# Zero-tile products on TensorE in thin stretches, later first loads of the MLP weights, and new order constants for head sets 25 to 39, in a transformer block scheduled by its own planner

## The chip, the cores and the metric

One core of one Trainium2 chip. The metric is device microseconds of one execution. The kernel before took 816.97 us (median of 3 runs, 816.37 to 817.6).

## The reference

One adaLN-conditioned transformer block on 2048 tokens of width 640, all in bf16: layer norm, an attention of 32 heads of width 20, and a bilinear gated MLP of inner width 1536. Six vectors of width 640 made from the condition c shift, scale and gate the two halves.

```python
mod = (silu(c) @ w_mod).reshape(1, 6, 1, 640)
sa, ca, ga, sb, cb, gb = mod[:, 0..5]
h = layernorm(x) * (1 + ca) + sa
q, k, v = heads(h @ wqkv)                   # 32 heads of 20
o = softmax(q k^T / sqrt(20)) v
x = x + ga * (o @ wo)
h = layernorm(x) * (1 + cb) + sb
x = x + gb * (((h @ w_gate) * (h @ w_up)) @ w_down)
```

## The kernel before

**Tiles.** Heads go in eight sets of four; the queries go in five chunks (CHUNKS: 512, 512, 512, 256, 256). A pair of chunk and set is an item, called a head set here: 40 of them, numbered 0 to 39 in the order in which they run. Items 0 to 23 belong to the 512-query chunks, 24 to 31 to the first 256-query chunk, 32 to 39 to the second. Scores are products of 32 rows of KT with QT (L1443, four row tiles of the array side by side), written to PSUM with keys on partitions. Most score tiles go through ScalarE, one exp over two or three banks at a time (L1479, into PP). Some, in groups of four called quads, go through VectorE by an arithmetic exp: four bank reads (L1503, into DB), then two masks and one product over 2048 columns (L1535, L1543, L1540, into DSS). QUADS says how many quads each item has. The value products (L2000, four column tiles of 32 columns) add all of an item into one PSUM bank, the value-product bank BPV. When an item is done, VectorE transposes that bank (L1627), takes a reciprocal (L1631), GpSimd scales (L1633), VectorE transposes again (L1641, into OcT), and small DMAs on SP's queue move the rows to Ocp (L1654).

**Per chunk, a suffix.** When its eight items are done, a chunk goes through the output projection (wo with Ocp, L906; L902 in the last chunk), residual, layer norm, transposes (L1758), gate and up products with weights loaded from DRAM into three stage buffers (stg, loads at L1798), their product (hprod) and the down projection (wd with hprod). This work is spread between the scores of the next chunk. The last chunk's suffix comes after the last scores.

**What sets the order.** A planner in the kernel file (class Sched) simulates the engines with costs of its own, picks what each engine does next, and so writes one fixed instruction order per engine; every engine then runs its list in order and waits on semaphores. SP's queue is such a list too: DMA issues stand behind each other. A DMA may have a gate, a number of score groups that must have started before it may be picked; gb is the number of the first group of the next chunk. For TensorE, pick_pe chooses: scores first, then, if recent activity in the planner's account of the last 3413 ns (HAM_W) is under FILL_MIN, other work, then value products in batches, then MLP and projection work, and last a fill: four identity products into a free bank (do_fill, L2329). Each item can set constants of its own (STAGE): batch sizes of value products (PVMIN, PVMAX, PVCAP), how long to hold for a score (HOLD, X_LATE), how far ahead quads are scored (DL, D_LATE, D_RES, EAGER) and FILL_MIN. Constants of item n hold while TensorE's value products are those of item n; DL of an item moves the due places of its own quads.

**Names that the steps touch.** KPB: staging of query rows on their way to DRAM (cast at L1178, written by L1212 to q_rows) and back (L1234, into QT). The stage loads of chunk 0 (L1798) have gate gb - 10. The first product that needs them starts at 268.3 us.

Of the kernel before, what the change touches and what calls it, by code (L numbers as in the profile page):

```python
# [8 lines left out]
BF16 = mybir.dt.bfloat16  # L9
# [7 lines left out]
PV_W = 216.0  # L17
# [100 lines left out]
class Sched:  # L118

    def __init__(self):  # L120
        self.tasks = []
        self.order = {k: [] for k in ("sp", "act", "pe", "dve", "pool")}
        self.all = []
        self.free_at = {k: T0 for k in self.order}
        self.pend = {k: [] for k in self.order}
        self.readyl = {k: [] for k in self.order}
        self.t = 0.0
        self.n = 0
        self.progress = 0
        self.dma_free = 0.0  # L130
        self.pe_mode = None
        self.pe_end = 0.0
        self.pick_pe = None
        self.every = []
        self.ham_w = 0
        self.ham_act = 0.0
        self.cold = True
        self.ncold = 0
        self.nfill = 0
        self.ndup = 0  # L140
        self.nsteal = 0
        self.nx = 0
        self.ng = 1 << 30
        self.hist = []
        self.acts = []
        self.left = 0
        self.lk_end = {"dve": 0.0, "pool": 0.0}
        self.lk_last = None
# [172 lines left out]
def emit_program(nc, sched, nsem_dma=56):  # L321
# [83 lines left out]
    with nc.Block() as block:  # L405
# [20 lines left out]
        def _(e):  # L426
# [5 lines left out]
QUADS = ((0, 4, 3, 3, 3, 3, 4, 4),  # L432
         (3, 4, 2, 4, 3, 4, 4, 4),
         (3, 3, 4, 4, 3, 4, 4, 4),
         (1, 2, 1, 2, 2, 1, 1, 1),
         (1, 1, 1, 1, 1, 1, 1, 1))
D_LEAD = 0.451
NB0, NSS = 2, 3
# [47 lines left out]
GATE_F = (0.468, 0.693, 0.969, 0.732, 1.0)  # L486
FILL_MIN = 4153.722
FILL_HARD = 0.0
FILL_T0, FILL_TH, FILL_MINH = 2300.0, 17000.0, 7500.0
FILL_MODE = 'P'  # L490
DUP_MIN = 0.0
# [37 lines left out]
    22: {"PVMAX": 7, "FILL_MIN": 3913.503, "D_RES": 17, "X_LATE": -76.434, "EAGER": 6, "D_LATE": 16, "PVCAP": 13},  # L529
    23: {"PVTOL": 247, "PVMAX": 7, "D_RES": 23},  # L530
    24: {"PVCAP": 13, "PVMAX": 7, "PVMIN": 2, "FILL_MIN": 4085.526, "DL": 0.464, "EAGER": 7, "STEAL_GAP": 200, "HOLD": 231},
    25: {"STEAL_GAP": 200, "HOLD": 144, "X_LATE": 22.894, "D_RES": 10, "FILL_MIN": 4068.834, "DL": 0.549, "PVCAP": 15, "D_LATE": 14},
    26: {"D_RES": 15, "X_LATE": -39.384, "PVMAX": 9, "PVCAP": 14, "STEAL_GAP": 200, "DL": 0.411},
    27: {"DL": 0.473, "D_LATE": 6, "PVMAX": 6, "EAGER": 6, "D_RES": 75, "PVTOL": 249, "PVMIN": 2, "X_LATE": -47.659},
    28: {"PVCAP": 13, "HOLD": 166, "X_LATE": 82.94},
    29: {"PVCAP": 14, "EAGER": 5, "PVMAX": 7, "D_RES": 46},
    30: {"X_LATE": -110.495, "PVCAP": 15, "FILL_MIN": 3782.61, "D_LATE": 16, "PVTOL": 292},
    31: {"D_RES": 19, "FILL_MIN": 4905.173, "D_LATE": 15, "PVMIN": 2, "X_LATE": 36.868},
    32: {"PVMIN": 2, "D_LATE": 17, "D_RES": 78},
    33: {"STEAL_GAP": 199.702, "D_LATE": 18, "PVCAP": 14, "PVMAX": 4, "DL": 0.442, "PVTOL": 353, "D_RES": 17, "PVMIN": 2, "HOLD": 100},  # L540
    34: {"X_LATE": 150, "D_LATE": 22, "HOLD": 117},
    35: {"PVMIN": 2, "PVMAX": 8, "FILL_MIN": 4516.564, "STEAL_GAP": 179.748, "X_LATE": -53.091, "HOLD": 151, "D_LATE": 12, "PVCAP": 14},
    36: {"PVMIN": 2, "D_RES": 10, "DL": 0.524, "X_LATE": -6.364, "FILL_MIN": 4156.61, "PVMAX": 8, "HOLD": 33},
    37: {"D_LATE": 12, "PVTOL": 254, "PVCAP": 13, "FILL_MIN": 4699.279},
    38: {"D_RES": 60, "PVMAX": 7, "PVTOL": 450, "HOLD": 67, "D_LATE": 16},
    39: {"FILL_MIN": 3000, "D_LATE": 17, "PVTOL": 258, "X_LATE": -54.236, "PVCAP": 16},
}
XHALF = 1
X_LATE = -24.052
X_HALF = 0.0  # L550

# [9 lines left out]
def build_kernel(nc, A_x, A_wqkv, A_wo, B_x, B_w_gate, B_w_up, B_w_down, c, w_mod, out):  # L561
# [29 lines left out]
    def alloc(name, shape, dtype):  # L591
        off = cur[0]
        cur[0] += nb(shape, dtype)
        assert cur[0] <= nc.sbuf_top, f"SBUF overflow at {name}: {cur[0]} > {nc.sbuf_top}"
        return at(name, shape, dtype, off)
# [25 lines left out]
    ident = alloc("ident", [128, 128], BF16)  # L621
    mhalf = alloc("mhalf", [128, 4], F32)
    warm = alloc("warm", [128, 1], F32)
    qcol = alloc("qcol", [128, 1], F32)
    c5 = alloc("c5", [KD, 128], BF16)
    csb = alloc("csb", [128, KD], BF16)
# [125 lines left out]
    def dve(dur, f, deps=(), prio=3.0, **k):  # L752
        return sc.add(Task("dve", dur, f, deps, prio=prio, **k))
# [6 lines left out]
    def pool(dur, f, deps=(), prio=3.0, **k):  # L760
        t = Task("pool", dur, f, deps, prio=prio, **k)
        t.lk = 1
        return sc.add(t)
# [63 lines left out]
    def load_rest():  # L827
# [5 lines left out]
        for q, f in enumerate((first2[0], first2[1],  # L833
# [13 lines left out]
    p_id = pool(300, lambda e: e.affine_select(ident[:], ident[:], pattern=[[-1, 128]], compare_op=ALU.not_equal,  # L847
                                               fill=1.0, base=0, channel_multiplier=1), [p_i0], prio=0)
    p_mh = pool(100, lambda e: e.memset(mhalf[:], -0.5), prio=1)
    p_on = dve(600, lambda e: e.memset(Vf[:, :].rearrange("p (h w) -> p h w", w=VW)[:, :, 0:1], 1.0), prio=-1)  # L850
    d_pz = dve(500, lambda e: e.memset(ps[:, BPV, :], 0.0), [], prio=3.5)
    d_wz = [dve(70, lambda e, w=w: e.memset(w[:, :, D:WKQ], 0.0), prio=0) for w in (wk_sb, wq_sb)]
# [824 lines left out]
    def suffix(ci):  # L1677
# [24 lines left out]
        def pr(early=False):  # L1702
            return pbase + rc_[0] - (1500 if tail and early else OPFIRST if early else 0)
        d_xc = dma("sp", 128 * ntl * D * 2, lambda e: e.dma_start(xck[:, 0:ntl, :], xv[:, t0:t0 + ntl, :]),
                   (first if alt else bd.get("out", []) + v_last), prio=15, gate=max(0, gb - 20))
        t_xn2 = []
        x1_done = []
        op_last = []
# [80 lines left out]
        for fc in range(FT):  # L1789
            use_x = tail and fc < nsx  # L1790
            wbuf, dm = [], []
            for w_, wv in enumerate((wgv, wuv)):
                cell = {}
                if use_x:
                    cell["t"] = stx[fc][:, w_, :, :]

                def f(e, wv=wv, fc=fc, cell=cell):
                    return e.dma_start(cell["t"], wv[:, :, fc * 128:(fc + 1) * 128])  # L1798
                t = dma("sp", 2 * 128 * KD * 128 * 2, f, sfx_done["qdead"] if use_x and fc < nsq else first if use_x else kp_use if ci == 0 else [], prio=16 + ci + .01 * fc,
                        gate=int(gstart[NC] - 40) if tail and not use_x else 0 if tail else max(0, gb - 10))  # L1800
                if not use_x:
                    t.acq = [(sStg[w_], "s", 1)]

                    def on0(task, cell=cell, w_=w_):
                        cell["i"] = task.slots["s"]
                        cell["t"] = stg[cell["i"]][:, w_, :, :]
                    t.on_start = on0
                wbuf.append(cell)
                dm.append(t)
# [112 lines left out]
    def mode_start(mode, t):  # L1922
        if sc.pe_mode is not None and sc.pe_mode != mode:
            return max(t, sc.pe_end + (PE_BACK if sc.pe_mode == 'S' else PE_SWITCH))
        return max(t, sc.pe_end)

    def s_ready():
        g = pvstate["sidx"]
        if g >= NG:
            return None  # L1930
        ts, us = score_q[g]
        r = 0.0
        for d in ts.deps:
            if d.done is None:
                return None
            r = max(r, d.done + SEM)
        for pool, key, refs in ts.acq:
            a = pool.avail()
            if a is None:
                return None  # L1940
            r = max(r, a[0])
        return r
# [265 lines left out]
    def pick_pe(t):  # L2208
# [99 lines left out]
        if cands and not js and len(cands) >= 2 and (not PV0 or it >= PV0N or len(cands) >= PV0 or cands[0][0] == 'd'):  # L2308
            pv_issue(cands, t)
            return True  # L2310
        if t > FILL_T0 and fill_ok(t, fill_deps):
            return do_fill(t)
        return False

    def do_fill(t):
        mode = FILL_MODE if pvstate["sidx"] else "X"
        start = mode_start(mode, t)
        fs = G
        if pvstate["sidx"] == 0:
            fs = next((q for q in (GX, GC) if q.avail() is not None and q.avail()[0] <= t), GC)  # L2320
        task = Task("pe", 216.0, ffill, fill_deps, ctr="pex", mode=mode, name="fill", acq=[(fs, "g", 1)])
        if not sc.acquire(task, t):
            return False
        b_ = task.slots["g"]
        idb = ident[:].unsqueeze(1).to_broadcast([128, 4, 128])
        if mode == "X":
            task.emits = [lambda e: e.matmul(ps[:, b_, :].rearrange("p (a b) -> p a b", a=4), ident[:], idb)]  # L2327
        else:
            task.emits = [lambda e, x=x: e.matmul(  # L2329
                ps[32 * x:32 * x + 32, b_, :].rearrange("p (a b) -> p a b", a=4), ident[:, 32 * x:32 * x + 32], idb,  # L2330
                tile_position=(0, 32 * x), skip_group_check=True) for x in range(4)]
        sc.activity(start, 512.0)
        sc.left += 1
        sc.finish_issue(task, start, 216.0 * clk())
        fs.done(b_, task)
        sc.pe_mode = mode
        sc.pe_end = start + 216.0 * clk()
        sc.free_at["pe"] = sc.pe_end
        sc.nfill += 1
        return True  # L2340
# [4 lines left out]
    def fill_ok(t, fdeps):  # L2345
        if any(d.done is None or d.done + SEM > t for d in fdeps):
            return False
        if xcur[0] is not None and not (PASSDEP or HT0_SPLIT):
            return False
        return sc.recent(t) < (FILL_MINH if t < FILL_TH else FILL_MIN)  # L2350
# [54 lines left out]
```

## Time and profile before

| | |
|---|---|
| Runs without profile | 816.97 us (816.37 to 817.6) |
| Profiled execution, first to last instruction | 821.3 us (the only time that is known of it) |
| ScalarE busy | 775.3 us, 94% |
| TensorE busy | 793.6 us, 97% (matmuls overlap, their ends are modelled) |
| VectorE busy | 720.4 us, 88% |
| Mean granted TensorE clock | 0.988 |
| exp on ScalarE (L1479) | 677 over two banks (1120 ns mean), 98 over three (1523 ns) |
| VectorE's read of a bank (L1503) | 400, 682 ns mean |
| masks and product of a quad (L1535, L1543, L1540) | 706, 690 and 1226 ns mean |
| identity fills (L2329) | 300 matmuls in groups of four |

The page's second part cuts the span into 40 slices with the busy share of each engine in tenths; the row PEclk is the granted clock of TensorE. The groups of part 5 give busy time, the mean of one, and the idle time ahead of them with what ended it. A line of the timeline gives start, length, engine, line, operation, tiles, count of merged instructions, and in brackets the idle time ahead with its releaser; SPq is the issue of a DMA by SP. A line of the windows view gives for a stretch its length, then for PE, PEld, DVE, ACT and POOL the busy time and count, then granted clock, DMA share and GB/s.

### The profile page before, as it was taken

What the parts mean: (1) busy time and instruction counts of PE and PEld (TensorE: products, weight loads), DVE (VectorE), ACT (ScalarE), POOL (GpSimd) and SP (SyncE); (2) the same over time, 40 slices, a digit from 0 to 9 for tenths busy, and PEclk for the clock granted to TensorE, in tenths of its full rate; (3) what the DMA queues carried; (4) which work ended last, traced back from release to release, by engine and by line L of the source; (5) the groups of instructions that cost most, each with busy time, mean ns of one, the idle gap of its engine ahead of it and who ended that gap; (6) DMA issues with size and microseconds to landing.
All of it is one profiled execution on the core that took longest, in us unless ns stands there. A gap on an engine that the chain in (4) does not pass through costs nothing.

```text
span 821.3 us, 28879 instructions
## 1 busy us (share of the span) xinstructions
PE 793.6 (97%) x12493; PEld 305.9 (37%) x12493; DVE 720.4 (88%) x1275; ACT 775.3 (94%) x818; POOL 79.1 (10%) x105
## 2 busy tenths in 40 slices
PE   9999999999989999999999999999988999999998
PEld 4433333322223223233233232333143444554567
DVE  7989999899989999999999999998798877667753
ACT  6899999999989999999999999999899999999941
POOL 3300000020002000000011000000011000001000
PEclk9999999999999999999999999999699999999999
DMA  9734211114500235000300222000400236105610
GB/s 292 219 85 104 67 45 40 50 33 123 131 18 25 54 99 138 22 11 23 92 7 6 53 54 54 6 21 23 82 8 10 50 87 134 47 30 127 137 42 17
DMA packets 116445, 54.71 MB, mean 67 GB/s; under 512 B 83915, under 2 KB 116319, under 8 KB 116319
## 3 DMA queue, kind: packets, MB, share of 16 engines
q1 hardware_dynamic: 115391, 51.72, 24.9%
q8 instruction: 99, 1.62, 0.8%
q10 hardware_dynamic: 928, 1.15, 0.4%
q14 instruction: 27, 0.22, 0.1%
HBM read 41.85 MB, written 8.41 MB: 61 GB/s over the span
## 4 chain that ended last, share of the span: by engine, by line
PE 43%; ACT 35%; DVE 15%; issue 7%; DMA 0%; SPq 0%; POOL 0%; DVEq 0%; ACTq 0%; POOLq 0%
ACT PP L1479 34%; PE ps_all L1443 13%; PE ps_all L906 13%; PE ps_all L2000 9%; DVE DB L1503 5%; PE ps_all L902 3%; DVE DSS L1540 3%; DVE DSS L1543 2%; DVE DSS L1535 1%; PE ps_all L2327 1%; PE ps_all L1166 1%; PE ps_all L1102 1%; PE ps_all L1063 1%; DVE wd L1429 1%; DVE gsb L1847 1%
## 5 line engine op out<-in xcount | busy, mean ns | idle before, releaser
L1479 ACT ACTIVATE PP<-ps_all 128x1024 bf16<-128x1024 f32 (+1 forms) x775 | 756.2, 1171 | 11.6 <-PE ps_all L1443 10.0
L1443 PE MATMUL ps_all<-QT,KT 32*128 32x512 bf16 (+1 forms) x2560 | 311.4, 343 | 16.6 <-ACT PP L1479 10.9
L1503 DVE TENSOR_SCALAR DB<-ps_all 128x512 int16<-128x512 f32 x400 | 265.0, 682 | 43.7 <-PE ps_all L1443 42.9
L1443 PEld LDWEIGHTS ps_all<-QT,KT 32*128 32x128 bf16 x2560 | 81.3, 91 | 264.9 <-ACT PP L1479 228.4
L2000 PE MATMUL ps_all<-PP,Vf 128*32 128x512 bf16 (+2 forms) x2084 | 166.0, 346 | 0.4 <-DVE OT L1627 0.4
L1540 DVE TENSOR_TENSOR DSS<-DB,DSS 128x2048 bf16<-128x2048 bf16 x100 | 122.6, 1226 | 0.0
L906 PE MATMUL ps_all<-h2T,stg 128*32 128x512 bf16 (+1 forms) x1740 | 116.8, 347 | 0.9 <-DVE DB L1503 0.2
L1633 POOL TENSOR_TENSOR OTn<-OT,invT 128x512 bf16<-128x512 f32 (+1 forms) x39 | 46.6, 1195 | 604.5 <-DVE invT L1631 604.5
L2000 PE MATMUL ps_all<-DSS,Vf 128*32 128x512 bf16 (+3 forms) x952 | 78.5, 354 | 1.0 <-DVE DSS L1540 0.5
L2000 PEld LDWEIGHTS ps_all<-PP,Vf 128*32 128x32 bf16 (+1 forms) x2084 | 46.0, 94 | 89.8 <-issue 82.0
L1535 DVE TENSOR_SCALAR DSS<-DB 128x2048 int16<-128x2048 int16 x100 | 70.6, 706 | 0.8
L1543 DVE TENSOR_SCALAR DSS<-DB 128x2048 int16<-128x2048 int16 x100 | 69.0, 690 | 0.3 <-PE ps_all L2000 0.3
L906 PE MATMUL ps_all<-wd,hprod 128*32 128x320 bf16 (+1 forms) x1316 | 58.5, 284 | 0.1
L906 PEld LDWEIGHTS ps_all<-h2T,stg 128*32 128x32 bf16 x1740 | 39.2, 96 | 35.0 <-issue 18.2
L906 PEld LDWEIGHTS ps_all<-wd,hprod 128*32 128x32 bf16 x1316 | 31.2, 96 | 16.6 <-issue 7.4
L2000 PEld LDWEIGHTS ps_all<-DSS,Vf 128*32 128x32 bf16 (+1 forms) x952 | 24.0, 95 | 25.1 <-issue 14.3
L906 PE MATMUL ps_all<-wV,hT 128*32 128x320 bf16 (+1 forms) x704 | 32.3, 289 | 0.1
L1166 PE MATMUL ps_all<-hT,wq 128*32 128x512 bf16 x375 | 31.6, 382 | 0.1
L906 PE MATMUL ps_all<-wo,Ocp 128*32 128x320 bf16 (+1 forms) x628 | 28.6, 290 | 1.9 <-DMA Ocp<-OcT 1.8
L2329 PE MATMUL ps_all<-ident 128*32 128x512 bf16 x300 | 28.6, 406 | 0.3 <-DVE DB L1503 0.2
L1847 DVE CAST gsb<-ps_all 128x512 bf16<-128x512 f32 x36 | 24.5, 681 | 3.0 <-PE ps_all L906 3.0
L1627 DVE STREAM_TRANSPOSE OT<-ps_all 128x512 f32<-128x512 f32 (+1 forms) x40 | 24.1, 603 | 2.8 <-PE ps_all L2000 2.7
(122 smaller groups left out, 509.1 us busy)
## 6 DMA issues: line engine op xcount, KB each, us to landing
stg<-in_B_w_gate_dram SPq DMA_DIRECT2D x50, 160.0 KB
stg<-in_B_w_up_dram SPq DMA_DIRECT2D x50, 160.0 KB
QT<-q_rows SPq DMA_DIRECT2D x22, 128.0 KB
KT<-k_rows SPq DMA_DIRECT2D x84, 32.0 KB
wm<-in_w_mod_dram SPq DMA_DIRECT2D x3, 800.0 KB
x<-in_A_x_dram SPq DMA_DIRECT2D x7, 320.0 KB
xck<-in_A_x_dram SPq DMA_DIRECT2D x3, 640.0 KB
wd<-in_B_w_down_dram SPq DMA_DIRECT2D x1, 1920.0 KB
```

The lines of the kernel that those rows point to most:

```text
L906: return lambda e, b: e.matmul(ps[32 * x:32 * x + 32, b, c0 + o:c0 + o + w], lhs()[:, 32 * x:32 * x + 32], rhs() if w == n else rhs()[:, o ...
L1166: f = [lambda e, b_, k=k, x=x: e.matmul(ps[x:x + min(32, w - x), b_, :], wx[:, k, r0 + x:r0 + min(x + 32, w)], hT[tc][:, k, :], tile_posit ...
L1443: ems.append(lambda e, i=i, kt=kt: e.matmul(dstf()[:, i * u.n:(i + 1) * u.n], KT[32 * u.s:32 * u.s + 32, u.j, kt * 128:(kt + 1) * 128], QT ...
L1479: return e.activation(PPs[g % 2][:, cellp["p"], 0:nu * 512], ps[:, b0:b0 + nu, :].rearrange("p b c -> p (b c)"), AFT.Exp, scale=ESCALE)
L1503: return e.tensor_scalar(DB0[:, st_["slot"], x * 512:(x + 1) * 512], bank(cell["b"]), EBIAS, 0.0, op0=ALU.add, op1=ALU.max)
L1535: return e.tensor_scalar(DSS[:, st_["ss"][0], :], DB0[:, st_["slot"], :], 0x7F, 0x3F00, op0=ALU.bitwise_and, op1=ALU.bitwise_or)
L1540: return e.tensor_tensor(d, DB0[:, st_["slot"], :].bitcast(BF16), d, ALU.mult)
L1543: return e.tensor_scalar(DSS[:, st_["ss"][1], :], DB0[:, st_["slot"], :], 0x7F80, 2, op0=ALU.bitwise_and, op1=ALU.bitwise_or)
L1633: f3 = lambda e: e.tensor_tensor(OTn[:, 0:n].rearrange("p (b c r) -> p b r c", c=32, r=2), OT[:, 0:n].rearrange("p (b r c) -> p b r c", c= ...
L1847: f = lambda e: e.tensor_copy(gsb[:, gs, 0:n], ps[:, r.b["b"], 0:n])
L2000: ems.append(lambda e, i=i, kt=kt, stt=stt, stp=stp: e.matmul(ps[32 * s:32 * s + mc, BPV, 0:u.n], Vf[:, (kt * H + 4 * u.j + s) * VW:(kt * ...
L2329: task.emits = [lambda e, x=x: e.matmul(ps[32 * x:32 * x + 32, b_, :].rearrange("p (a b) -> p a b", a=4), ident[:, 32 * x:32 * x + 32], id ...
```

## The change

It adds zero_fill: when pick_pe finds nothing else, and the planner's recent activity is under FILL_Z (of 3300, or an item's own value), and the next score is not made late by it, four products of a 128x32 tile of zeros (zt) with the identity are added to the value-product bank of the item under way. They need no bank of their own and change no value. The first stage loads of chunk 0 get gate gb + 12 in place of gb - 10. Item 31 gets a second quad. The constants of items 25 to 39 are set anew.

In the orders that result, TensorE's is the same as before up to about 572 us of the profile of before; from there on it differs, above all in chunks four and five. There are two zero fills in all, eight matmuls: the first in a run of score products at about 572.5 us, between a batch of five and one of two, the second at about 624 us, ahead of three transposes of the third chunk's suffix. Identity fills go from 300 matmuls to 284. ScalarE's exps go from 677 over two banks and 98 over three to 676, 97 and one over a single bank. VectorE gets 404 bank reads for 400 and 101 quads for 100. In the last chunk's suffix, 180 down-projection matmuls of chunk four stand between the output projection and the transposes, where there were 144, and 12 more behind the transposes. On SP's queue the writes of KPB, the two reads of QT and the four copies to Ocp at the end of chunk 0 now stand ahead of the six stage loads, which stood ahead of them.

```diff
-         (1, 2, 1, 2, 2, 1, 1, 1),
+         (1, 2, 1, 2, 2, 1, 1, 2),
...
+FILL_Z, Z_LATE = 3300.0, 0.0
...
-    28: {"PVCAP": 13, "HOLD": 166, "X_LATE": 82.94},
-    29: {"PVCAP": 14, "EAGER": 5, "PVMAX": 7, "D_RES": 46},
...
+    28: {"PVCAP": 13, "HOLD": 166, "X_LATE": 82.94, "D_RES": 26, "PVMIN": 1, "FILL_Z": 3201.704, "FILL_MIN": 4200.542, "PVTOL": 224, "Z_LATE": -31.227},
+    29: {"PVCAP": 15, "EAGER": 6, "PVMAX": 7, "D_RES": 55, "FILL_Z": 3606.407, "FILL_MIN": 4442.563},
...
+STG_G0, STG_G, XC_G = 12, -10, -20
...
+    p_zt = pool(100, lambda e: e.memset(zt[:], 0.0), prio=5) if FILL_Z > 0.0 else None
...
-                        gate=int(gstart[NC] - 40) if tail and not use_x else 0 if tail else max(0, gb - 10))
+                        gate=int(gstart[NC] - 40) if tail and not use_x else 0 if tail else max(0, gb + (STG_G0 if ci == 0 else STG_G)))
...
-        if t > FILL_T0 and fill_ok(t, fill_deps):
-            return do_fill(t)
-        return False
+        if t > FILL_T0 and fill_ok(t, fill_deps) and do_fill(t):
+            return True
+        return FILL_Z > 0.0 and sc.recent(t) < FILL_Z and zero_fill(t)
+
+    def zero_fill(t):
+        it = st_pv["item"]
+        if it >= len(items) or pvstate["sidx"] < 2 or not item_info[it]["started"] or t < FILL_TH or p_zt.done is None:
+            return False
+        start = mode_start("P", t)
+        sr = s_ready()
+        if sr is not None and start + PV_W > sr + Z_LATE:
+            return False
+        idb = ident[:].unsqueeze(1).to_broadcast([128, 4, 128])
+        task = Task("pe", 216.0, [lambda e, x=x: e.matmul(
+            ps[32 * x:32 * x + 32, BPV, :].rearrange("p (a b) -> p a b", a=4), zt[:], idb,
+            tile_position=(0, 32 * x), start=False, stop=False, skip_group_check=True) for x in range(4)],
+            [p_zt, p_id], ctr="pep", mode="P", name="zfill")
+        task.seq = 0
+        sc.activity(start, 512.0)
...
```

## The prediction

> **What bounds the kernel now.** I read the page's slices first: from the third slice to the 38th ScalarE stands at 9 tenths, except in slices 12 and 29, and in the second of these PEclk drops as well.
>
> ```profile
> ACT  6899999999989999999999999999899999999941
> PEclk9999999999999999999999999999699999999999
> ```
>
> So the exps set the pace, and time is lost where they pause. Next the windows view in long stretches (length; PE, PEld, DVE, ACT, POOL busy; granted clock; DMA):
>
> ```profile
> 60.00:220.00 160.00, 157.42 (x2140) 48.86 (x2137) 150.01 (x245) 159.29 (x175) 12.76 (x8) 1.00 0.26 69
> 220.00:240.00 20.00, 17.33 (x225) 5.11 (x217) 16.57 (x26) 17.33 (x20) 1.81 (x1) 0.91 0.36 74
> ...
> 560.00:600.00 40.00, 36.66 (x474) 10.83 (x474) 32.21 (x50) 36.83 (x34) 2.43 (x2) 0.83 0.25 55
> 600.00:640.00 40.00, 36.63 (x716) 17.17 (x712) 36.62 (x74) 38.71 (x35) 6.41 (x12) 0.96 0.06 14
> 640.00:785.00 145.00, 141.29 (x3210) 71.37 (x3206) 105.59 (x196) 144.99 (x129) 10.39 (x16) 1.00 0.39 86
> ```
>
> ScalarE pauses in three stretches, and those are the ones with a clock under 1.00. In the timeline of ScalarE the pauses end with score products (the bracket); the first two places, with what stood on SP's queue at the first:
>
> ```profile
> 219.87 0.44 SPq L1798 DMA_DIRECT2D stg<-in_B_w_gate_dram  x1
> ...
> 223.24 1.26 SPq L1212 DMA_DIRECT2D q_rows<-KPB  x2
> ...
> 227.16 0.83 SPq L1234 DMA_DIRECT2D QT<-q_rows  x2
> ...
> 228.03 3.05 SPq L1654 DMA_DIRECT2D Ocp<-OcT  x4
> ...
> 232.33 0.73 PE L906 MATMUL ps_all<-wo,Ocp 128*32 128x320 bf16 x16 [1.76 <-DMA Ocp<-OcT]
> ...
> 233.65 1.02 ACT L1479 ACTIVATE PP<-ps_all 128x1024 bf16<-128x1024 f32 x1 [1.69 <-PE ps_all L1443]
> ```
>
> ```profile
> 577.39 1.02 ACT L1479 ACTIVATE PP<-ps_all 128x1024 bf16<-128x1024 f32 x1 [0.48 <-PE ps_all L1443]
> 578.91 2.53 ACT L1479 ACTIVATE PP<-ps_all 128x1536 bf16<-128x1536 f32 x2 [0.50 <-PE ps_all L1443]
> ```
>
> *Place 1* (231.9 to 236.7): TensorE, in order, waits 1.76 us for the copies to Ocp, then runs 3.41 us at clock 0.50. ScalarE's pauses: 1.69 + 0.59 + 0.39 = 2.67. *Place 2* (574.3 to 588.0): 13.65 us at 0.50, six pauses, 0.48 + 0.50 + 0.50 + 0.50 + 0.48 + 0.61 = 3.07. *Place 3* (629.0 to 632.4): 3.41 us at 0.50, one pause of 1.29. Between 640 and 785 ScalarE is busy 144.99 of 145.00. An exp alone takes 1.02 us, 16 in a row 14.94, so (14.94 - 1.02)/15 = 0.93 each: a pause costs 0.09 more than its gap. Places: 2.67 + 3 x 0.09 = 2.9; 3.07 + 6 x 0.09 = 3.6; 1.29 + 0.09 = 1.4.
>
> **Why the clock halves there.** The clock records are 3.413 us long or four times that. I cut the span on their grid and weighted each matmul of the trace by its tile (32x128 or 128x32: a quarter of the array) and its moved columns; a full window would hold 8192. The windows ahead of the three drops hold 2561, 2810 and 2986; after 60 us no other window at full clock is under 3150. Window 2 by the windows view:
>
> ```profile
> 567.51:570.93 3.42, 3.18 (x51) 1.00 (x43) 3.15 (x6) 3.42 (x5) 0.53 (x1) 1.00 0.00 0
> 570.93:574.34 3.41, 2.79 (x27) 0.76 (x26) 3.38 (x6) 3.41 (x4) 0.00 (x0) 1.00 0.20 65
> 574.34:577.75 3.41, 3.41 (x27) 0.54 (x26) 3.21 (x5) 2.93 (x4) 0.00 (x0) 0.50 0.43 83
> ```
>
> 27 matmuls after 51, TensorE busy 2.79 of 3.41: thin work, not standstill, halves the clock. The Trainium skill (TensorE: Matmul & The Clock Gate, the table of "Why this matters for your kernels") says otherwise: it asks only that TensorE have no gap over about 3 us. Here the longest gap was 1.76 us and the clock fell, so the trace disagrees; by that rule the zero products would be useless (rival 1).
>
> **The change, part by part.**
>
> *Stage loads later.* Six issues of about 0.53 us (219.87 to 223.15) leave the way of the KPB writes. KPB is cast at 221.50. Writes 1.26, to 222.8; the wait for their landing, 2.66 before (224.50 to 227.16), 2.25 for an earlier pair without such loads in the queue; two QT reads 0.83 and issue gaps 0.05, to 225.9 to 226.3; OcT is ready at 224.0; four copies 3.05, to 229.0 to 229.4; last landing 1.24 after (231.09 to 232.33 before): 230.2 to 230.6. TensorE needs it at 230.57, so the wait of 1.76 falls to 0 to 0.1, the window holds more than 3150, and place 1 goes: **-2.9** (at least -1.8, the wait without the clock). Behind the late loads on SP nothing is due until 244.5; their first user starts at 268.3, 35 us of cover.
>
> *First zero product.* It adds 512 to the 2810: 3322. It sits where TensorE idled 0.52 us ahead of the score products at 573.30; four fills take 0.40 (the L2329 rows). **-3.6**, if the fill counts as work. For it: identity fills, nearly all zeros too, are about half of the 3112 in the window (584.6 to 588.0) after which the clock came back. If the 0.40 is not hidden, it costs that much, for each of the two; I take 0.
>
> *Second zero product and the order around it.* +512 in or next to the thin window of place 3, and eight gate/up products now split the run of 18 score products: **-1.4**.
>
> *Quad in item 31.* Four banks less on ScalarE. 129 exps alternating two and three banks (322 banks) in 145.0 us are 0.450 each: **-1.8**. VectorE gains 4 x 0.682 + 0.706 + 0.690 + 1.226 = 5.4 us in a stretch where it is busy 105.6 of 145.0: hidden, else up to +5.4 spread over the stretch. TensorE's extra value products, 8 net of 0.27 us four abreast, are 0.5 us.
>
> *Tail.* Before, the last transposes began 6.28 us after the first OcT product (790.65 to 796.93), with 144 down products between, 4.94 us for 140 (0.035 each); LN had ended at 796.38, so TensorE was the later. Now 180: 36 x 0.035 = 1.27 more, less about 0.6 since the four OcT products stand together (the fourth came 1.17 after the first, 0.4 would do); the evacuations after it, three on VectorE instead of two, save some 0.2. **+0.4** (-0.3 to +1.3).
>
> *Redrawn constants.* The longest TensorE work between two score batches, counted from the order, is 1.17 us at four abreast, 1.07 before; two exps of two and three banks take 2.25. I cost them at 0, between -0.5 and +2.
>
> Sum: -2.9 - 3.6 - 1.4 - 1.8 + 0.4 = -9.3 of the span, 821.3 to 812.0. The runs are 4.3 below the span of the profiled execution, and no view says where. It may be a constant, or place 2: its thin stretch, with the exps laid back to back, is only about 1.5 us of window starts wide (571 to 572.5), against 3.413, so if the grid lies elsewhere in another execution it hits in under half of them. Places 1 and 3 are about 3 us wide and hit nearly always. I charge place 2 at half: 9.3 - 1.8 = 7.5, **816.97 - 7.5 = 809.5**. The skill's same page (Part 1) says that the window is free-running and does not reset with the kernel; no run here shows it, and by it 3.6 is the price in some executions and 0 in others.
>
> **The rivals.**
>
> 1. *Zero products do not hold the clock*, or thinness is not the cause. For: nothing here shows a product of zeros alone. Against: the identity fills above. Then place 1 and the quad stay: 2.9 + 1.8 - 0.4 = 4.3, 812.7.
> 2. *The Ocp copies stay late*, so the change does not do what it says at place 1: SP's landing wait is 2.66 or more and my margin is 0.4. Then 7.5 - 2.9 = 4.6: 812.4.
> 3. *TensorE becomes the bound* from 600 us on. It is busy 141.3 of 145.0 there, 3.7 us to spare, and the order is new. If scores come late by 0.06 us on average over 130 exps, 7.8 us, the gain is gone; at 0.1, 13 us, less 7.5: slower by 5, 822.5. Against: between 640 and 785 scores were never waited for, and the work between batches is hardly longer.
> 4. *Much smaller gain*: rival 3 in part, 816.5.
>
> **How the numbers follow.** Forecast 809.5, 0.64 (own range 806.5 to 812.2: place 2 paid whole gives 807.7, not at all 811.3, and the tail and the constants add -1.2 to +0.9); rival 1 0.14, rival 2 0.09, rival 4 0.07, rival 3 0.06. Range 805.8 to 814: it holds the forecast and rivals 1 and 2 and leaves out the others. A measurement of this kernel tells about 0.2% (1.6 us) from no change. Faster 0.87, same 0.07, slower 0.06.
>
> **What would show it.** Right: PEclk at 9 from the first slice on; no wait of L906 wo,Ocp for a DMA near 230; ScalarE without pauses over 0.3 us from 62 us to its last exp, which ends some 9.7 us earlier; about 33 us from there to the end. Wrong: low clock behind a zero product (rival 1), a wait for Ocp left (rival 2), or ScalarE waiting for score products between 600 and 785 at full clock (rival 3).

## The result, and the profile after

The changed kernel takes 814.94 us (median of 13 runs, 814.88 to 816.18), the kernel before 817.67 in the 13 runs beside it (815.34 to 822.97). The ratio is 0.9956, 95% interval 0.9939 to 0.9972: faster by 0.44%, some 3.6 us by the ratio, 2.7 by the medians. The forecast was 809.5, the range began at 805.8 and ended at 814.0, so the time lies 0.9 above it. The sign was right, and the size was not.

The profiled execution of the changed kernel took 815.03 us with a span of 813.2. Span against span that is 821.3 - 813.2 = 8.1 less, close to the 9.3 that I had summed. The page of the changed kernel, ScalarE and the granted clock in the 40 slices:

```profile
ACT  7899999999999999999999999999999999999941
PEclk9999999999999999999999999999999999999999
```

Both dips of before, slices 12 and 29, are gone. The windows view of the changed kernel, with the columns of the one shown for before:

```profile
220.00:240.00 20.00, 18.94 (x268) 5.98 (x266) 19.45 (x33) 20.00 (x23) 3.02 (x3) 1.00 0.32 69
...
560.00:600.00 40.00, 35.55 (x584) 13.19 (x584) 36.01 (x61) 40.00 (x36) 3.80 (x5) 1.00 0.24 52
600.00:640.00 40.00, 36.24 (x725) 16.69 (x720) 37.41 (x70) 39.80 (x36) 6.39 (x10) 1.00 0.09 22
640.00:776.00 136.00, 131.24 (x2964) 66.21 (x2968) 101.17 (x186) 135.59 (x120) 9.36 (x15) 1.00 0.38 86
```

ScalarE is busy 20.00 of 20 where it had 17.33, 40.00 of 40 where it had 36.83, and the clock is 1.00 in all of them. SyncE's queue at place 1 in the changed kernel (the copies to Ocp now stand ahead of the stage loads):

```profile
221.00 1.25 SPq L1217 DMA_DIRECT2D q_rows<-KPB  x2
224.10 0.81 SPq L1239 DMA_DIRECT2D QT<-q_rows  x2
224.95 3.07 SPq L1659 DMA_DIRECT2D Ocp<-OcT  x4
228.06 0.48 SPq L1803 DMA_DIRECT2D stg<-in_B_w_gate_dram  x1
```

The four copies are issued by 228.0, where I had 229.0 to 229.4. So each edit stands in the trace where I had said, and the signs that the prediction named for being right are there too: no clock drop, no wait of the first wo,Ocp product for a DMA, no pause of the exps over 0.27 us from 62 us on, and a last exp that ends 9.1 earlier (9.7 named). From the first exps to the end of the last one, the profiled execution is 8.6 shorter (before, 27.28 to 788.52; now 26.77 to 779.44). What fails is the step from that execution to the runs: 8.1 between two spans, 2.7 between two medians. Two runs stand far apart from the others of their kernels and are left out of all figures below: 2212.93 of b_zero and 852.11 (clock 0.851) of c_nq.

### The profile page after: what moved, and what is told of

It reads as the page before. It is cut to its first block, busy times and chain, and to the rows that moved or that the text cites. A ratio compares the mean times of both kernels' runs of the same rounds, so it can differ in the third digit from the quotient of the medians.

```text
span 813.2 us, 28869 instructions
## 1 busy us (share of the span) xinstructions
PE 785.0 (97%) x12485; PEld 305.5 (38%) x12485; DVE 724.7 (89%) x1283; ACT 772.8 (95%) x816; POOL 79.4 (10%) x106
## 4 chain that ended last, share of the span: by engine, by line
PE 47%; ACT 34%; DVE 12%; issue 6%; POOL 0%; DVEq 0%; ACTq 0%; POOLq 0%
ACT PP L1484 34%; PE ps_all L911 16%; PE ps_all L1448 14%; PE ps_all L2005 10%; DVE DB L1508 5%; PE ps_all L907 3%; DVE DSS L1545 2%; DVE DSS L1548 1%; DVE DSS L1540 1%; PE ps_all L1171 1%; PE ps_all L1107 1%; PE ps_all L2355 1%; PE ps_all L1068 1%; DVE wd L1434 1%; DVE OT L1632 1%
## 5 line engine op out<-in xcount | busy, mean ns | idle before, releaser
L2005 PE MATMUL ps_all<-PP,Vf 128*32 128x512 bf16 (+2 forms) x2076 | 163.5, 343 | 0.0
L2005 PE MATMUL ps_all<-DSS,Vf 128*32 128x512 bf16 (+1 forms) x968 | 77.9, 348 | 0.9 <-DVE DSS L1545 0.5
L2005 PEld LDWEIGHTS ps_all<-DSS,Vf 128*32 128x32 bf16 x968 | 24.3, 95 | 24.5 <-issue 15.0
L1863 DVE TENSOR_TENSOR hprod<-ps_all,gsb 128x512 bf16<-128x512 f32 x36 | 24.4, 678 | 3.3 <-PE ps_all L911 3.3
L2357 PE MATMUL ps_all<-ident 128*32 128x512 bf16 x284 | 25.7, 384 | 0.3 <-DVE DB L1508 0.2
```

Source lines behind the costliest of these rows:

```text
L2005: ems.append(lambda e, i=i, kt=kt, stt=stt, stp=stp: e.matmul(ps[32 * s:32 * s + mc, BPV, 0:u.n], Vf[:, (kt * H + 4 * u.j + s) * VW:(kt * ...
L2357: task.emits = [lambda e, x=x: e.matmul(ps[32 * x:32 * x + 32, b_, :].rearrange("p (a b) -> p a b", a=4), ident[:, 32 * x:32 * x + 32], id ...
```

## The experiments

All kernels start from the kernel before ("b") or the changed one ("a", "c"). Beside its time, each run lists its span and its mean granted clock. A window is one stretch of 3.41 us on the grid of the clock records; one at half clock takes 3.41/2/815 = 0.002 from the mean. The experiments ran on several chips, and runs of the kernel before stood beside each. Its runs at clock 1.000 have a median of 815.02 beside x_before, b_late, a_noz and b_quad, 814.98 beside b_zero, c_mix27, a_zid and a_tiny, 814.62 beside a_early, b_lz and a_noquad, and 815.20 beside c_nq. So differences of half a microsecond hold only within one of these groups.

**The kernel before, once more** (x_before), no edit.

> The kernel before, once more, to read the granted clock of run after run. Theory A (the half-clock windows hit only some executions, since the thin stretches lie differently on the 3.413 us grid each time): the mean clock scatters between 0.987 and 1.000, and the time goes with it, some 3.6 us for 0.008 (13.65 us at half clock); the run with the least lost is near 815.3. Theory B (every execution loses the same three places, and the spread has another cause): the clock is 0.987 or 0.988 in every run and the spread of 7.6 us does not go with it.

Median 817.12 (814.48 to 822.38), as Theory A has it. With the runs of before that stood beside all the kernels below, 122 runs of it, sorted by their clock:

```
mean clock        runs   median us   from - to
1.000 (0.9995+)    36     814.94     814.30 - 815.87
0.997, 0.998       43     816.61     815.72 - 817.73
0.996 and less     43     818.90     816.88 - 825.01
```

The time follows the clock: a line through the 122 gives 0.35 us for each us at half clock, correlation 0.93. 36 runs lose no window at all, and their median is the changed kernel's. Six of the 122 are at 0.988 or less; the execution that I had read (three drops, 20.5 us at half clock, 0.988 on its page) was one such. And time less span is 1.75 to 1.85 in every one of them: the runs were not "4.3 below the span" by a constant. By that, the execution with the span of 821.3 would be a run of about 823.1.

The page of this second profiled execution (819.39 us, clock 0.992) has its dip of the clock in slice 29 too, 7 tenths where the first had 6:

```profile
PEclk9999999999999999999999999999799999999999
```

Place 2 runs 10.24 us at half clock there (three windows; four in the first trace). The other window at half clock, from 633.82 on, is not place 3 but a fourth thin stretch eight exps behind it, which the prediction does not have; ScalarE pauses 1.26 there, at place 3 of the first trace 1.29. The exps behind the two pauses, the first trace ahead:

```profile
632.87 8.23 ACT L1479 ACTIVATE PP<-ps_all 128x1536 bf16<-128x1536 f32 x7 [1.29 <-PE ps_all L1443]
```

```profile
637.50 2.37 ACT L1479 ACTIVATE PP<-ps_all 128x1536 bf16<-128x1536 f32 x2 [1.26 <-PE ps_all L1443]
```

Place 1 is without its wait. SyncE's queue, then TensorE's products on Ocp:

```profile
218.19 0.53 SPq L1798 DMA_DIRECT2D stg<-in_B_w_up_dram  x1
218.76 1.44 SPq L1798 DMA_DIRECT2D stg<-in_B_w_gate_dram  x1
...
222.01 1.25 SPq L1212 DMA_DIRECT2D q_rows<-KPB  x2
225.54 0.82 SPq L1234 DMA_DIRECT2D QT<-q_rows  x2
226.41 3.07 SPq L1654 DMA_DIRECT2D Ocp<-OcT  x4
```

```profile
230.73 0.46 PE L906 MATMUL ps_all<-wo,Ocp 128*32 128x320 bf16 x8 [0.22 <-DMA Ocp<-OcT]
```

One issue takes 1.44 in place of 0.53, but the copies are issued from 226.41 on, not 228.03, and TensorE waits 0.22, not 1.76. The first trace has such an issue too (1.38, at 218.44). What set it apart is that SyncE was 1.2 late already from 209.0 on (0.5 from before 206.3, and 0.7 by another long issue, 1.36 in place of 0.67 at 206.73), and that the KPB writes landed slower (2.66 against 2.28). Place 1 is a matter of 1 to 2 us of luck on SyncE.

**The later stage loads alone** (b_late).

```diff
-  gate=... max(0, gb - 10))
+  gate=... max(0, gb + (12 if ci == 0 else -10)))
```

> The kernel before with only the six stage loads asked for later; the order on every other engine is the same. If place 1 costs its wait in every execution and its clock in nearly all, the median falls by 1.8 to 2.9, to 815.0 to 816.0, and the fastest run falls too, to 812.5 to 813.5. If the wait of 1.76 us for Ocp is not there, or is made good later, in an execution at full clock, the fastest run stays at 815.3 and the median moves by less than 1.

Median 815.42 (814.33 to 818.56), ratio 0.9986 (0.9965 to 1.0008), so by itself not told from no change. Six runs at clock 1.000 have a median of 815.06; four at 0.998, 815.85; two at 0.992, both 818.56. The median is 1.4 under the 816.84 of before beside it, inside the 815.0 to 816.0 expected if place 1 struck nearly always; but the fastest run, 814.33, is that of before, 814.31, and at clock 1.000 the two do not differ (815.06 against 815.02). The 2.9 are not there in every execution.

**The changed kernel with early loads again** (a_early) asks the same from the other side.

```diff
-STG_G0, STG_G, XC_G = 12, -10, -20
+STG_G0, STG_G, XC_G = -10, -10, -20
```

> The changed kernel with the six stage loads ahead of the KPB writes again; every other engine's order is the same, so only place 1 is open. Theory: in most executions the copies to Ocp still land in time (as in the second profile of the kernel before, where TensorE did not wait), and the time stays at 814.9 to 815.1; in a quarter of them, where one of SP's issues takes 1.4 to 1.8 us in place of 0.5, the wait and one half-clock window cost 2 to 3 and the mean clock is 0.998. Median 814.9 to 815.3, slowest run 817 to 818.5. Rival, the prediction's term: place 1 costs 1.8 to 2.9 in nearly all executions: median 816.8 to 817.9.

Median 815.06 (814.69 to 819.26), ratio to before 0.9999 (0.9986 to 1.0012) in a group in which before had 12 of 29 runs at clock 1.000. Ten runs at clock 1.000 (814.69 to 816.17, median 814.96), one at 0.998 (817.94), one at 0.996 (819.26). So place 1 in full (3 to 4.3 us) came in 2 of 12; at full clock the rest spread by up to 1.2 above their median, as parts of the wait would give (not shown: no trace of such a run). The prediction's term, in nearly all executions, is refuted.

**Without the zero products** (a_noz).

```diff
-FILL_Z, Z_LATE = 3300.0, 0.0
+FILL_Z, Z_LATE = 0.0, 0.0
```

(and every FILL_Z of a head set taken out)

> The changed kernel without its two groups of zero products, all else kept (one transpose stands elsewhere). If the zero products hold the clock: the fastest run is at 814.9 like the changed kernel's, but some runs show a mean clock of 0.998 to 0.988 and 1.4 to 5 us more; the median rises by 0 to 2.5 and the spread is above 3 us. If they hold nothing (rival 1, and the new order alone filled the thin stretches): all runs within 814.7 to 816.2, clock 1.000.

Median 815.02; eleven of 12 runs at 0.999 or 1.000 and 814.90 to 815.23, one at 0.994 with 817.60. So some runs do fall, but 12 runs with one fall cannot tell by themselves what the zero products do. The traces can. Weighted as in the prediction, a window that starts at the worst moment of place 2 holds 2563 in the trace of a_noz, and 3073 in that of the changed kernel. The highest window that a drop came after anywhere holds 2989 (below); in a_noz the starts of windows under 2990 are 1.3 us wide at place 2, in the changed kernel there are none. From 600 to 640 us, place 3 and the fourth stretch in it, the least is 2990 without the zero products and 2993 with them: there the new order is enough, and the second group is not needed. The one run at 0.994 lost three windows, as place 2 did in the second trace of before; it has no trace itself.

**One group of zero products alone** (b_zero): the kernel before with zero_fill, which places four zero products at place 2; the order otherwise as before, loads early, no quad. What changes in TensorE's list (with the shapes of the outputs):

```diff
 L1443 Matmult ps_all<-QT,KT 128x512 x5
+      Matmult ps_all<-ident,zt 32x512 x4
 L1443 Matmult ps_all<-QT,KT 128x512 x2
```

> The kernel before with one group of four zero products alone, at place 2 (between the fifth and the sixth of seven score products in a row); every other instruction stands as before, place 1 and place 3 included. If zero products hold the clock: the long drops at place 2 go (a mean clock of 0.996 or less, 16 of the 46 runs of before so far, at 817.0 to 825.0), those of 0.998 stay in about half of the runs; median 815.5 to 816.7, slowest run under 819.5. If they hold nothing: 3 to 6 of 12 runs at 0.996 or less, slowest run 819 to 823.

Median of eleven runs 815.44, ratio 0.9978 (0.9952 to 1.0005). Five are at 1.000 (median 814.40), three at 0.998 (815.62), three at 0.994 to 0.996 (818.58 to 819.05). By the count that I had named (runs at 0.996 or less) this is no decision: 3 of 11 against 43 of the 122 runs of before. Those three can be place 3 or the fourth stretch together with place 1 in full, which stay open here, but no trace shows it, and the one at 0.994 lost three windows. Place 2 alone loses three or four, so 0.994 or less is the mark to count by. Over all kernels with the zero group at place 2 and full-size fills (the changed kernel, a_early, a_zid, a_noquad, b_zero, b_lz, c_mix27, c_nq) it is 1 run of 93, and none is under 0.994; of before it is 38 of 122, and 26 are under 0.994. With the order otherwise untouched (b_zero, b_lz) it is 1 of 23. And the trace of b_zero has no window start at place 2 under 3074. So the zero products close place 2. At place 1, where the copies came in time although the loads were early, no window there holds less than 3584: that place is thin only when TensorE waits.

**Places 1 and 2 closed, 3 open** (b_lz): b_zero with the late loads (STG_G0 = 12).

> The kernel before with the late stage loads and the one group of zero products at place 2: places 1 and 2 are closed, only place 3 is open. In the profile of the kernel with the zero group alone, window starts with less than 2990 ahead of place 3 lie 1.6 us wide, of 3.413. Theory (the grid lies at random): 1.6/3.4, or about half, of the runs at mean clock 0.998 and some 1.4 us above the others, which are at 1.000 and 814.4 to 815.0; nothing at 0.996 or less, no run over 817. Rival (place 3 hits nearly always, as I had it): 0.998 in nearly all, median 816.0 to 816.4.

Median 814.43 (814.01 to 816.03), in two groups: eight runs at 1.000, 814.01 to 814.58 (median 814.10); four at 0.998, 815.41 to 816.03 (median 815.60). The price of place 3 is 1.5, as I had it (1.4); its share is 4 of 12 and not nearly all. Why I had the share too high: I had read the width of the thin stretches from a trace in which the clock had fallen there. There products run slower (the same four score products take 1.03 us at half clock, at 574.80 in the trace of before, and 0.61 in that of b_zero, at 571.57), so fewer fall into a window, and the thin stretch looks wider than it is. In the trace of b_lz, at full clock, the window starts under 2990 ahead of place 3 are 1.6 us wide, in the trace of before 3.25. The fourth stretch adds 0.3. That is over half of a grid of 3.41; 4 of 12 is less, but 12 runs do not tell the two apart.

**Products of zeros as fills** (a_zid), and **fills of 8 columns** (a_tiny). Both keep order and waits; what the fills write is not used.

```diff
-  ..., b_, :]..., ident[:, 32*x:32*x+32], idb     (4 x 512 columns)
+  ..., b_, :]..., zt[:], idb                      (a_zid)
+  ..., b_, 0:8], ident[:, 32*x:32*x+32], ident[:, 0:8]   (a_tiny)
```

> The changed kernel with the identity as stationary tile of the four-abreast filling products replaced by the zero tile: all fills of the main part are products of zeros. If a product counts for the clock by the columns it moves, whatever it multiplies: clock 1.000 and 814.9 to 815.2, no change. If a stationary tile of zeros counts for less than an identity: half-clock windows about the fills, as in the kernel with fills of 8 columns, and 816 or more.

> The changed kernel with each four-abreast filling product moving 8 columns in place of 512; order and waits stay. The contrast for the kernel with zero fills: it shows what the fills are worth. If they hold the clock: windows of under 2990 appear at the fills between 165 and 660 us, each 3.4 us or more at half clock; mean clock 0.97 to 0.99, time 818 to 835. If they hold nothing: 814.9.

a_zid: 815.04 (814.91 to 815.32), clock 0.999 to 1.000 in all ten runs: a stationary tile of zeros holds the clock as the identity does. a_tiny: 833.11 (830.31 to 837.04), clock 0.941 to 0.954. The granted clock of a_zid, then of a_tiny:

```profile
PEclk9999999999999999999999999999999999999999
```

```profile
PEclk9999999999587999999876999999679999998999
```

Six stretches fall (the row shows them run together), 99 us at half clock in all, and no gap of TensorE in this trace is longer than 0.82 us after 65 us. So it is work for each window that counts, and rival 1 falls. The Trainium skill (TensorE: Matmul & The Clock Gate, "HAM oscillation — how this bites in real kernels") has the rule that TensorE should have no idle gap over about 3.4 us; this trace keeps it with a gap of 0.82 and takes 18 us longer all the same.

On the 3.413 us grid of all traces that have a drop to set it by, weighted as in the prediction, 13 drops at full clock came after windows of 2366 to 2989, none after one above; between 2723 and 2989 eleven windows were not followed by a drop. The edge is near 2900, about 35% of a full window (in the changed kernel's trace products of 512 columns over the whole array start 0.215 to 0.217 us apart at full clock, so 3.413 us hold some 8100). It is not sharp in this weighting, which counts the columns of a product up to its end. Counted from its start, the 13 drops come after windows of 2216 to 2895, and the lowest window without a drop behind it holds 2901.

**The quad alone** (b_quad).

```diff
-         (1, 2, 1, 2, 2, 1, 1, 1),
+         (1, 2, 1, 2, 2, 1, 1, 2),
```

> The kernel before with only the added quad (item 31, last entry 1 to 2), which draws the order of items 31 to 39 anew; the half-clock windows stay. By the prediction's term the time falls by 1.8 (four banks of 0.450 on ScalarE): median 815.9, fastest 813.5. If the quad is worth nothing, because TensorE or the tail gives it back: median 817.7 and fastest 815.3, with ScalarE done some 1.8 earlier and the tail 1.8 longer, or ScalarE waiting between 690 and 785.

Median 815.81 (813.83 to 820.71), ratio 0.9988 (0.9963 to 1.0013); four runs at clock 1.000, median 814.16, against 815.02 of before on that chip. ScalarE ends earlier, and the end after it grows from 32.76 (b_late, no quad) to 33.73. TensorE at the end of b_late, whose last exp ends at 781.09:

```profile
789.50 0.73 PE L1758 MATMUL ps_all<-ident,xn2c 128*128 128x128 bf16 x10
791.35 4.87 PE L902 MATMUL ps_all<-h2Tc,stx 128*128 128x256 bf16 x43 [1.12 <-ACT h2Tc L1765]
```

and of b_quad, whose last exp ends at 780.46:

```profile
789.26 0.73 PE L1758 MATMUL ps_all<-ident,xn2c 128*128 128x128 bf16 x10
789.93 1.81 PE L906 MATMUL ps_all<-wd,hprodt 128*32 128x320 bf16 x48
791.67 4.54 PE L902 MATMUL ps_all<-h2Tc,stx 128*128 128x256 bf16 x40
```

The transposes begin 8.8 after the last exp, not 8.4: the last value products, those on the quads' DSS among them, end 0.9 after it and not 0.5. Then 48 down products are left over and hold the first gate products: 11.2 after the last exp, not 10.3.

**Old constants from head set 28 on** (c_mix27): the changed kernel with the rows 28 to 39 of the table as before; and the same **without the quad** (c_nq).

```diff
-    28: {"PVCAP": 13, "HOLD": 166, "X_LATE": 82.94, "D_RES": 26, ...},
+    28: {"PVCAP": 13, "HOLD": 166, "X_LATE": 82.94},
 ...
```

> The changed kernel with the constants of head sets 28 to 39 as they were before; late stage loads, quad and both groups of zero products stay, and so does the new order at place 3. Theory: at full clock the quad is worth 0.9 (the kernel before with the quad alone: 814.16 at clock 1.000, against 815.0) and the redrawn constants of the late head sets give it back by scores that come 20 to 190 ns late and a longer end: median 814.1, clock 1.000. Rival: what the changed kernel lost against the quad alone lies in the zero products or the late loads: median 814.9 to 815.0, as the changed kernel.

> The kernel with the constants of head sets 28 to 39 as before (late loads, both zero groups, the new order at place 3), now without the quad as well. All three places are closed, so clock 1.000 in every run. If the quad is worth 0.5 to 0.9 net (ScalarE 1.8 less, the end 1.0 longer): 814.8 to 815.2 against 814.34 with it. If nearly all of it is eaten: 814.1 to 814.5. By the prediction's term of 1.8 alone: 816.1.

c_mix27: 814.34 (814.19 to 814.70), clock 1.000 in all 12 runs, ratio to before 0.9957 (0.9935 to 0.9979); a_zid, which times like the changed kernel, took 815.04 on the same chip, 0.7 more. It is the lowest median here (b_lz, 814.43 on another chip, is not told from it). c_nq: 814.77 in eleven runs, all at 1.000, ratio 0.9967 (0.9946 to 0.9988). So the quad is worth some 0.4 by the medians; set against the runs of before at clock 1.000 beside each, 0.6 and 0.4 under them, it is 0.2. In the traces the exps take 1.44 less (from the ninth exp to the end of the last one 753.45 without, 752.01 with), and the end 0.88 more (32.82 and 33.70), which leaves 0.6.

**The changed kernel without the quad** (a_noquad), the edit of b_quad turned round.

> The changed kernel without its added quad. If the quad is worth 0.9 here too (ScalarE 1.8 less, the end 1.0 longer, as in the kernel before with the quad alone): 815.8 to 815.9, clock 1.000, the end after the last exp near 32.8. If its 1.8 are eaten by scores that come late under the redrawn constants: 814.9 to 815.2, and fewer late exps without it. By the prediction's term alone: 816.7.

Median 816.31, ratio to before 1.0002 (0.9988 to 1.0016), clock 1.000 in ten of 12, yet in two groups, four at 815.26 to 815.32 and six at 816.27 to 816.91. In the profiled run, of the second group, the last exp waits 0.83 for its scores:

```profile
779.87 1.45 ACT L1484 ACTIVATE PP<-ps_all 128x1536 bf16<-128x1536 f32 x1 [0.83 <-PE ps_all L1448]
```

Whether that makes the two groups stays open. Against a_early on the same chip (814.96 at clock 1.000), leaving the quad out costs 0.3 in the first group and 1.6 in the second: the constants were drawn for an order with it.

## Why the prediction was wrong, step by step

**The step that failed is the one from the profiled execution to the runs.** It read: "The runs are 4.3 below the span of the profiled execution, and no view says where. It may be a constant, or place 2", and "Places 1 and 3 are about 3 us wide and hit nearly always. I charge place 2 at half". I charged 2.9 + 1.4 + 1.8 = 6.1 us of clock and wait to the median run. Each run is 1.8 above its own span, so the execution that I read was a run of about 823.1, and the three runs beside it (816.37 to 817.6) already lacked most of what I meant to remove. The median run of before has one window at half clock. The median of the 122 is 1.9 above the runs without any (816.79 against 814.94), and that is most of the 2.7 that the median gained; the 13 runs of before beside the changed kernel have no clock on record. With the 1.8 known, the spans say it at once: 821.3 + 1.8 = 823.1 against a median of 816.97 leaves 6.1 of the 7.9 us of the three places out of a typical run. That the difference of the spans, 8.1, comes near the 9.3 is in part luck: a profile without the drops would have shown nothing to gain at the three places.

*Stage loads, -2.9:* size right where it strikes, share wrong: in full in 2 of 12 (a_early), perhaps in parts in more; nothing at clock 1.000 on one chip (b_late 815.06, before 815.02).

*First zero product, -3.6, half of it charged:* it closes place 2. A drop there costs 3.5 (b_late, 818.56 against 815.06) and came in 2 of 12 runs there; 26 of the 122 runs of before are at 0.993 or less. With the 12 at 0.994, which lost three windows, it is 38. So it is a fifth to a third and not a half, and a median hardly sees it. The 0.39 us of the group cost nothing: b_zero at full clock is not slower than before at full clock (814.40 against 814.98 on the same chip). Why it is 0.6 lower there stays open.

*Second zero product and its order, -1.4:* price right (1.5), share a third (4 of 12, the fourth stretch in it). The order does it (2990 at the least without the zero products, 2993 with them).

*Quad, -1.8, and tail, +0.4:* ScalarE gains 1.44, and the end loses 0.9 by the quad itself, which I had looked for in the 36 down products. Net 0.2 to 0.6 with the old constants of the late head sets (c_nq), 0.9 in the four runs of b_quad at clock 1.000. In the changed kernel the end after the last exp is 1.0 longer than before (33.8 and 32.8).

*Redrawn constants, 0 (-0.5 to +2):* +0.7 for those of head sets 28 to 39, within the bounds. From about 680 us on, the two-bank exps take some 0.96 us more in sum than in c_mix27, from one start to the next, only 0.3 of it as waits for scores that the profile shows; how the rest arises is open. The prediction's own range left their upper bound out: tail and constants add up to +2.9 at most, not +0.9, which would have ended it at 814.2 and not 812.2.

At clock 1.000 the changed kernel gains nothing: 815.01 against 815.02 of before on one chip (a_noz), 815.04 against 814.98 (a_zid), 814.96 against 814.62 (a_early). Its whole gain is the windows that it no longer loses. How the smaller terms cancel is shown only in part. *Rivals:* 1 falls (a_zid, a_tiny); 2 does not hold, as the copies are early; 3 does not hold either (the exps wait 0.3 us in sum from 680 us on), though the constants are a small piece of it. Rival 4, a much smaller gain (816.5), came nearest in size, but by another mechanism.

## What to carry to other kernels

Ahead of pricing a drop of the clock, compare the profiled execution's own time with the spread of the runs: a stall that hangs on where a window falls is worth its price times its share of the runs, and a profile in which it struck shows it at full price. Take the width of a thin stretch from a trace that did not fall there, since a fallen clock widens it. A filling product of zeros, placed where the engine idles, closed one such place here at no cost; the redrawn order must then pay for itself separately, and here its late part did not (c_mix27, with the old constants of head sets 28 to 39, takes 0.7 less than a_zid).

## What the runs showed of the hardware

- *The grid lies differently in each execution.* The same program lost no window in 36 of 122 runs, and up to some 24 us at half clock in others (clock 0.985). Counted in windows of 3.413 us from the first instruction, the first drop of the traces of before, x_before, b_late, b_quad and a_tiny starts at 68.26, 167.69, 182.17, 182.40 and 62.39. The Trainium skill (TensorE: Matmul & The Clock Gate, Part 1) says that the window is free-running and doesn't reset when a kernel starts; these traces agree, since the fraction differs from one to the next. At 0.35 us for each us at half clock its price here is 0 to some 8.5 us.
- *Zeros count as work for the clock*: 815.04 with zero tiles in all four-abreast fills against 814.94, clock 0.999 to 1.000 in both.
- *A DMA issue on SyncE takes 1.0 to 2.4 us now and then*, against 0.4 to 0.8 for its like: 18 times in the first trace of before, 23 times in the second, eight at the same instructions and the rest at others (about 218.5 a QT read in the one, a stage load in the other). What causes it no run here tells.
